# Clustered attention with a mish feed-forward: scores from float16 pairs, with a scale per head

## The chip, the cores and the metric

The kernel runs on one core of one Trainium2 chip. Times are device microseconds (us) of one execution. TensorE (PE in the rows, PEld for its weight loads), VectorE (DVE), ScalarE (ACT), GpSimd (POOL) and SyncE (SP, which only issues transfers) each work through their own instructions in order, and wait for each other by semaphores.

## What is computed

Four batches of eight heads, 768 positions, 64 elements a head. Each query and each key belongs to one of 16 clusters of its head; a query sees only the keys of its own cluster. Then a feed-forward layer with x·tanh(softplus(x)) ("mish").

```python
q_assign = argmax(einsum('bhsd,hcd->bhsc', q_n, c_n))      # q_n, k_n, c_n: unit length
k_assign = argmax(einsum('bhsd,hcd->bhsc', k_n, c_n))
mask = q_assign[:, :, :, None] == k_assign[:, :, None, :]
scores = where(mask, (q @ k.T) / 8, -1e9)
attn = softmax(scores)
x = (attn @ v)                                             # to (3072, 512)
h = x @ w_in                                               # w_in 512 x 2048
out = (h * tanh(softplus(h))) @ w_out                      # w_out 2048 x 512
```

## The kernel before

**Units.** The work on attention is cut into 96 units i (a head and 256 queries), each in two half units a (128 queries): 192 half units. Head n = i // 3; batch 0 is heads 0 to 7, units 0 to 23.

**Precision.** float32 values are split into a high and a low part, and products are built from parts. For a head's scores, `prep_hi` makes A, the rounded part of q (rows 0 to 63, times 0.125) and k (rows 64 to 127), and `prep_lo` makes B, what is left of both. `copy_t`, `copy_z`, `copy_b` and `copy_a` move halves of them about, so that the tiles B, A, T and Z hold what two products need: one with 128 rows (B and A) and one with 64 rows of parts and 16 rows of cluster marks (T and Z). All four are float32r, a 4-byte type. `hot_copy` writes the marks: where query and key share a cluster, 2^64 is added to the score. `scores(i, a)` issues four matmuls of 384 columns into one of two score banks (tag S): two of line L631 (B, A) and two of L636 (T, Z).

**Behind the scores.** `rowmax` (VectorE, L648) takes the negated maximum m of a row, `expo` (ScalarE, L662) exp(s + m) and its sum l, `total` and `recip` (VectorE, L674 and L682) one over the sum, `p_hi` (GpSimd, L700) the high part hl, `p_lo` (VectorE, L717) the low part, `ptrans` a transposing DMA into pt, `pv` (L753) the products with v, `pv_out` and `x_lo` the two parts of x. In batch 0 the probabilities stay float32 and are transposed by TensorE (L710).

**Clusters.** For each group q of four heads `assign_mm` multiplies raw q and k with the centroids, into a score bank; `assign_turn`, `assign_max`, `assign_hot` and `assign_back` on VectorE find the marks, `assign_put` and `assign_stg` turn them into values.

**Feed-forward.** `m1` (L832 to L834) forms h from x, `e_mish` (ScalarE, L843) applies mish, `e_gh` (GpSimd) and `e_gl` (VectorE, L857) split it, `m2` (L873 to L875) multiplies by w_out. ScalarE loads the table with mish before each pair of j, and the one with exp behind it (L842, L845). The feed-forward of a batch runs beside the attention of the next. The last two row blocks of the output use seven products in place of eight (L1025).

**What sets the order.** Every step has a due time from tables (T, N, and a shift for single steps). The program issues steps by due time, each behind the steps it needs, and so fixes the order on every engine. Nothing is reordered afterwards.

`norm_power` (L211 to L222) makes a power of two and its inverse from a sum: six operations on VectorE.

Of the kernel before, what the change touches and what calls it, by code (L numbers as in the profile page):

```python
# [8 lines left out]
F32 = mybir.dt.float32  # L9
# [12 lines left out]
BIG = float(2.0**64)  # L22
E20 = 485165195.40979
# [49 lines left out]
def tile_clustered_attention_mish_ffn(  # L73
# [36 lines left out]
    idle = cp.tile([P, 512], BF16, name="idle")  # L110
# [43 lines left out]
    def put_consts():  # L154
# [16 lines left out]
        )  # L171
    scq = cp.tile([P, 1], F32, name="scq")
# [38 lines left out]
    def norm_power(total, name, pool, tag, unit=2.0**-13):  # L211

        t = pool.tile([P, 1], F32, tag=f"{tag}t", name=f"{name}t")
        tu = t.bitcast(U32)
        nc.vector.tensor_scalar(t, total, 2.0**-120, None, op0=ALU.max)
# [3 lines left out]
        r = pool.tile([P, 2], F32, tag=f"{tag}r", name=f"{name}r")  # L219
        nc.vector.tensor_scalar(r[:, 1:], t, unit, None, op0=ALU.mult)  # L220
        nc.vector.reciprocal(r[:, :1], r[:, 1:])
# [245 lines left out]

    def operand(n, nm):
        st[nm, n] = opp.tile([P, S], F32R, tag=nm, name=f"{nm}_{n}")
        return st[nm, n]  # L470
# [5 lines left out]

    def prep_hi(n):
        pl.after(("qk_load", n))
        r, A = st["qk", n], operand(n, "A")
        if n < T["direct"]:  # L480
            nc.scalar.activation(A, r, AF.Copy, scale=scq)
            return
        if share(n, "f_b", n >= late):
            nc.gpsimd.tensor_scalar(r, r, scq, 1.0, op0=ALU.mult, op1=ALU.mult)
        sc = 1.0 if share(n, "f_b", n >= late) else scq
# [5 lines left out]
    def prep_lo(n):  # L491
        pl.after(("prep_hi", n))
        if n < T["direct"]:
            nc.vector.scalar_tensor_tensor(
                operand(n, "B"), st["qk", n], scq, st["A", n].bitcast(F32), op0=ALU.mult, op1=ALU.subtract
            )
            return
        r, A, Bt = st["qk", n], st["A", n].bitcast(F32), operand(n, "B")
        if share(n, "f_b", n >= late):
            nc.gpsimd.tensor_tensor(Bt, r, A, op=ALU.subtract)  # L500
        else:
            nc.vector.scalar_tensor_tensor(Bt, r, scq, A, op0=ALU.mult, op1=ALU.subtract)

    def copy(n, kind, dst, src):
        if n < T["direct"]:

            if kind != "copy_z":
                nc.scalar.copy(dst, src.bitcast(F32))
            else:
                nc.vector.tensor_copy(dst, src.bitcast(F32))  # L510
        elif share(n, f"f_{kind}", n >= late):
            nc.scalar.copy(dst, src.bitcast(F32))
        else:
            queue(n, kind).dma_start(dst.bitcast(F32), src.bitcast(F32))
# [61 lines left out]
    def assign_put(q):  # L576
        pl.after(("assign_back", q), ("put_consts",))
# [1071 lines left out]
```

## Time and profile before

| what | value |
|---|---|
| three runs | 871.47, 876.18, 876.86 us; median 876.18 |
| the profiled execution, its time | 873.17 us |
| its span (first to last instruction) | 871.44 us |
| TensorE busy | 838.5 us (96%) |
| weight loads busy | 608.8 us (70%) |
| VectorE busy | 697.9 us (80%) |
| ScalarE busy | 520.9 us (60%) |
| GpSimd busy | 434.9 us (50%) |

Matmuls overlap in their pipeline, so TensorE's busy time says that it had work, not how fast it went; for that one reads from the start of one matmul to the start of the next. The trace of this execution is the source of all rows below.

### The profile page before, as it was taken

What the parts mean: (1) busy time and instruction counts of PE and PEld (TensorE: products, weight loads), DVE (VectorE), ACT (ScalarE), POOL (GpSimd) and SP (SyncE); (2) the same over time, 40 slices, a digit from 0 to 9 for tenths busy, and PEclk for the clock granted to TensorE, in tenths of its full rate; (3) what the DMA queues carried; (4) which work ended last, traced back from release to release, by engine and by line L of the source; (5) the groups of instructions that cost most, each with busy time, mean ns of one, the idle gap of its engine ahead of it and who ended that gap; (6) DMA issues with size and microseconds to landing.
All of it is one profiled execution on the core that took longest, in us unless ns stands there. A gap on an engine that the chain in (4) does not pass through costs nothing.

```text
span 871.4 us, 17412 instructions
## 1 busy us (share of the span) xinstructions
PE 838.5 (96%) x6670; PEld 608.8 (70%) x6671; DVE 697.9 (80%) x1178; ACT 520.9 (60%) x881; POOL 434.9 (50%) x410
## 2 busy tenths in 40 slices
PE   8999899889999999999999999999999999999998
PEld 3666666667767767776777767776776777777787
DVE  7889988889978879778978789779888776488831
ACT  6878977667457567456556666465565555345520
POOL 1463656587657547466567457466566543110000
PEclk9999999999999999999999999999999999999999
DMA  8765671289679997688779997988967876000000
GB/s 322 254 181 153 187 220 46 61 166 188 126 141 173 214 179 134 135 180 168 136 135 182 195 171 128 159 178 148 156 130 141 144 131 122 13 1 14 2 31 32
DMA packets 253060, 121.51 MB, mean 139 GB/s; under 512 B 230288, under 2 KB 230800, under 8 KB 252976
## 3 DMA queue, kind: packets, MB, share of 16 engines
q1 hardware_dynamic: 247632, 108.46, 59.2%
q10 hardware_dynamic: 5344, 11.93, 6.7%
q8 instruction: 53, 0.87, 0.4%
q14 instruction: 31, 0.25, 0.1%
HBM read 35.72 MB, written 6.29 MB: 48 GB/s over the span
## 4 chain that ended last, share of the span: by engine, by line
PE 68%; DVE 14%; DMA 6%; ACT 5%; issue 3%; POOL 3%; ACTq 0%; SPq 0%; DVEq 0%; POOLq 0%
PE o L753 8%; PE h L832 8%; PE O L873 7%; PE h L833 7%; PE h L834 7%; PE O L875 7%; PE O L874 7%; PE s L631 5%; PE s L636 5%; DVE m L648 4%; DMA pt<-hl 3%; DVE hl L717 2%; ACT p L662 2%; DVE w L347 1%; PE as L543 1%
## 5 line engine op out<-in xcount | busy, mean ns | idle before, releaser
L662 ACT ACTIVATE p<-s,m 128x768 f32<-128x768 f32 x192 | 172.6, 899 | 173.5 <-DVE m L648 91.7
L700 POOL TENSOR_SCALAR hl<-p,l 128x768 f16<-128x768 f32 x144 | 172.2, 1196 | 149.2 <-DVE l L682 80.7
L648 DVE TENSOR_REDUCE m<-s 128x1 f32<-128x768 f32 x192 | 182.4, 951 | 39.7 <-PE s L636 35.8
L832 PE MATMUL h<-x,w 128*128 128x256 f16 x640 | 175.8, 275 | 4.0 <-ACT u L843 3.4
L717 DVE SCALAR_TENSOR_TENSOR hl<-p,l,hl 128x768 f16<-128x768 f32 x144 | 166.5, 1157 | 11.7 <-POOL hl L700 11.4
L833 PE MATMUL h<-x,w 128*128 128x256 f16 x640 | 174.4, 273 | 0.0
L834 PE MATMUL h<-x,w 128*128 128x256 f16 x640 | 174.4, 273 | 0.0
L631 PE MATMUL s<-A,B 128*128 128x384 f32 x384 | 119.0, 391 | 8.8 <-ACT p L662 6.1
L873 PE MATMUL O<-w,g 128*128 128x512 f16 x320 | 121.7, 380 | 0.0
L875 PE MATMUL O<-w,g 128*128 128x512 f16 x320 | 121.3, 379 | 0.0
L874 PE MATMUL O<-w,g 128*128 128x512 f16 x320 | 121.3, 379 | 0.0
L857 DVE SCALAR_TENSOR_TENSOR g<-u,mscg,g 128x512 f16<-128x512 f32 x80 | 92.0, 1150 | 35.8 <-POOL g L849 35.6
L849 POOL TENSOR_SCALAR g<-u,mscg 128x512 f16<-128x512 f32 x80 | 73.7, 924 | 66.9 <-ACT u L843 54.5
L636 PE MATMUL s<-Z,T 80*128 80x384 f32 x384 | 98.8, 338 | 1.9 <-DVE T L603 1.0
L832 PEld LDWEIGHTS <-w 128*128 128x128 f16 x768 | 75.1, 98 | 30.9 <-issue 19.6
L833 PEld LDWEIGHTS <-w 128*128 128x128 f16 x768 | 75.5, 98 | 15.6 <-issue 4.4
L753 PE MATMUL o<-pt,v 128*64 128x256 f16 x1296 | 79.3, 274 | 2.5 <-DMA pt<-hl 2.3
L834 PEld LDWEIGHTS <-w 128*128 128x128 f16 x768 | 75.1, 98 | 8.9 <-issue 0.2
L753 PEld LDWEIGHTS <-v 128*64 128x64 f16 x1296 | 68.5, 110 | 14.7 <-issue 12.2
L631 PEld LDWEIGHTS s<-A,B 128*128 128x128 f32 x384 | 61.3, 190 | 23.2 <-ACT p L662 9.4
L636 PEld LDWEIGHTS s<-Z,T 80*128 80x128 f32 x384 | 69.6, 189 | 2.5 <-ACT Z L600 1.3
L500 POOL TENSOR_TENSOR B<-qk,A 128x768 fp32r<-128x768 f32 x30 | 61.6, 2052 | 0.6
(225 smaller groups left out, 1299.9 us busy)
## 6 DMA issues: line engine op xcount, KB each, us to landing
qk<-in_qk_dram SPq DMA_DIRECT2D x32, 384.0 KB, 4.7
stage<-in_w_in_dram SPq DMA_DIRECT2D x16, 512.0 KB, 6.8
stage<-in_w_out_dram SPq DMA_DIRECT2D x16, 512.0 KB, 4.5
vraw<-in_vP_dram SPq DMA_DIRECT2D x16, 384.0 KB, 6.3
T<-A ACTq DMA_DIRECT2D x30, 192.0 KB, 3.3
Z<-B SPq DMA_DIRECT2D x30, 192.0 KB, 3.1
B<-T ACTq DMA_DIRECT2D x28, 192.0 KB, 3.5
out_dram<-osb SPq DMA_DIRECT2D x20, 256.0 KB, 2.7
```

Source lines behind the costliest of these rows:

```text
L631: nc.tensor.matmul(s[:, j, :384], st["B", n][:, q0 : q0 + P], st["A", n][:, j * 384 : (j + 1) * 384], start=True, stop=False,)
L636: nc.tensor.matmul(s[:, j, :384], st["T", n][: D + NCL, q0 : q0 + P], st["Z", n][: D + NCL, j * 384 : (j + 1) * 384], start=False, stop=True,)
L648: nc.vector.tensor_reduce(m, st["s", i, a][:, :, :384], axis=AX.XY, op=ALU.max, negate=True)
L662: nc.scalar.activation(p.rearrange("p (n x) -> p n x", n=2), st["s", i, a][:, :, :384], AF.Exp, bias=st["m", i, a], scale=1.0, accum_out=l,)
L717: nc.vector.scalar_tensor_tensor(t[:, 1], p, r, t[:, 0], op0=ALU.mult, op1=ALU.subtract)
L753: nc.tensor.matmul(o[s * D : s * D + D, :256], v if early else v[:, int(part == 1)], st["pt", 2 * m + s][:, :, c + (0 if early or part < 2 ...
L832: nc.tensor.matmul(o, wh, xh, start=(c == 0), stop=False)
L833: nc.tensor.matmul(o, wh, xl, start=False, stop=False)
L834: nc.tensor.matmul(o, wl, xh, start=False, stop=(c == 3))
L873: nc.tensor.matmul(o, gh, wh, start=(f == 0 and fi == 0), stop=False)
L874: nc.tensor.matmul(o, gh, wl, start=False, stop=False)
L875: nc.tensor.matmul(o, gl, wh, start=False, stop=(f == 7 and fi == 1))
```

## The change

It holds for batches 1 to 3 (`narrow(n)`: heads 8 to 31, units 24 to 95, 144 half units). There A, B, T and Z are float16, a 2-byte type, and so are the marks' values; q and k of each head are first multiplied by powers of two.

The scale comes from a sum of squares: `q_sq` (new, ScalarE) sums the squares of each row of a head; `assign_sum` (new, TensorE) adds the rows of q and those of k by two small float32 matmuls with a constant tile of ones (`side`), into the spare columns of the group's cluster bank; `assign_scale` (new, VectorE) turns them by `norm_power` and one more operation into scales `qs` for the operands and `qu` for the scores. `put_more` (new, once) changes the constants of the marks from 2^64 to 2^15 and makes `side`. `prep_hi` and `prep_lo` take `qs` in place of the constant scale.

Between the row maximum and the exponential stands `level` (new, two operations on VectorE on 128x1): it makes a scale per row (zero where a row has no key of its cluster) and an offset, and the exponential takes both.

For j = 74, 76 and 78 the table with mish is no longer loaded again.

```diff
+    def narrow(n):
+        return gof[n] >= H
     def operand(n, nm):
-        st[nm, n] = opp.tile([P, S], F32R, tag=nm, name=f"{nm}_{n}")
+        st[nm, n] = opp.tile([P, S], F16 if narrow(n) else F32R, tag=nm, name=f"{nm}_{n}")
         return st[nm, n]
...
+    def q_sq(n):
+        pl.after(("qk_load", n))
...
+        junk = gp.tile([P, S], BF16, tag="g", name=f"qj{n}")
+        nc.scalar.activation(junk, st["qk", n], AF.Square, accum_out=st["qq", q][:, j : j + 1])
+
+    def assign_sum(q):
+        n0 = owner[q]
+        pl.after(("assign_mm", q), ("put_more",), *(("q_sq", n0 + j) for j in range(4)))
+        for k in range(2):
+            nc.tensor.matmul(
+                st["as", q][:, S + 4 * k : S + 4 * k + 4], st["side"][:, k].rearrange("p a d -> p (a d)"), st["qq", q],
+                start=True, stop=True, skip_group_check=True,
+            )
+
+    def assign_scale(q):
+        pl.after(("assign_sum", q))
+        r = norm_power(st["as", q][:, S : S + 8], f"qs{q}", sm, "qs", wide=8, least=2.0**8)
+        u = sm.tile([P, 4], F32, tag="qu", name=f"qu{q}")
+        nc.vector.scalar_tensor_tensor(u, r[:, 8:12], 0.125, r[:, 12:], op0=ALU.mult, op1=ALU.mult)
...
     def prep_hi(n):
         pl.after(("qk_load", n))
-        r, A = st["qk", n], operand(n, "A")
+        if narrow(n):
+            pl.after(("assign_scale", gof[n] // 4))
+        r, A, s = st["qk", n], operand(n, "A"), st["qs", n] if narrow(n) else scq
...
-        stg = op1.tile([P, S], F32R, tag="stg", name=f"stg{q}")
+        stg = op1.tile([P, S], F32R if q < 2 else F16, tag="stg", name=f"stg{q}")
...
+    def level(i, a):
+
+        pl.after(("rowmax", i, a))
+        m, u = st["m", i, a], st["qu", units[i][2]]
+        w = sm.tile([P, 2], F32, tag="mw", name=f"mw{i}_{a}")
+        eng = nc.vector if share(2 * i + a, "f_m", True) else nc.gpsimd
+        eng.tensor_scalar(w[:, 0:1], m, FAR, u, op0=ALU.is_lt, op1=ALU.mult)
+        eng.tensor_scalar(w[:, 1:2], m, w[:, 0:1], 1.0, op0=ALU.mult, op1=ALU.mult)
+        st["mw", i, a] = w
...
-            bias=st["m", i, a], scale=1.0, accum_out=l,
+            bias=bias, scale=scale, accum_out=l,
...
-        if j % 2 == 0:
+        if j % 2 == 0 and j <= 72:
             nc.scalar.preload_act_table_set("mish")
...
-    'scores': 1.895,
-    'rowmax': -0.3,
+    'scores': 6.714,
+    'rowmax': 0.767,
+    'level': -0.29,
```

`share(..., "f_m", True)` is always true (the table has 1), so every `level` is VectorE's. The tables of due times change throughout (the last lines of the diff show three entries); on TensorE nearly all steps keep their places in batch 0, and from batch 1 on some change them. Three places follow.

TensorE, the second half unit of unit 54 (`s54_1`; O is a block of `m2`, h one of `m1`). Before:

```order
L874 MATMUL O3_0_5066<-w11_1101,g13_4945 128x512
L875 LDWEIGHTS g13_4945
L875 MATMUL O3_0_5066<-w11_1101,g13_4945 128x512
L631 MATMUL s54_1_5260<-A_18_4839,B_18_4994 128x384 x2
L636 MATMUL s54_1_5260<-Z_18_4996,T_18_4925 128x384 x2
L832 LDWEIGHTS w6_610
L832 MATMUL h30_5227<-x1_0_0_2468,w6_610 128x256
```

Of the change, the same place:

```order
L895 LDWEIGHTS w6_608
L895 MATMUL h30_5485<-x1_3_0_4563,w6_608 128x256
L678 LDWEIGHTS B_18_5269
L678 MATMUL s54_1_5506<-A_18_5066,B_18_5269 128x384
L683 LDWEIGHTS T_18_5179
L683 MATMUL s54_1_5506<-Z_18_5271,T_18_5179 128x384
L934 LDWEIGHTS g13_5187
L934 MATMUL O3_0_5319<-w10_980,g13_5187 128x512
```

(Each of the two LDWEIGHTS and MATMUL pairs of the scores stands there twice.) The scores moved from behind the twelve matmuls of O3_0 to ahead of them; and a float16 weight load is an instruction of its own.

VectorE from the first half unit of unit 54 on (m the maximum, l the sum, hl the parts of the probabilities, g those of mish). Before:

```order
L648 TENSOR_REDUCE m54_0_5224<-s54_0_5219 128x1
L717 SCALAR_TENSOR_TENSOR hl53_1_5242<-p53_1_5205,l53_1_5206,hl53_1_5242 128x768
L648 TENSOR_REDUCE m54_1_5265<-s54_1_5260 128x1
L674 TENSOR_SCALAR l54_0_5268<-l54_0_5268 128x1
L682 RECIPROCAL l54_0_5268<-l54_0_5268 128x1
L857 SCALAR_TENSOR_TENSOR g14_5156<-u29_5160,mscg1_4596,g14_5156 128x512
L648 TENSOR_REDUCE m55_0_5294<-s55_0_5289 128x1
```

Of the change:

```order
L695 TENSOR_REDUCE m54_0_5479<-s54_0_5474 128x1
L704 TENSOR_SCALAR mw54_0_5481<-m54_0_5479,qu4_4373 128x1
L705 TENSOR_SCALAR mw54_0_5481<-m54_0_5479,mw54_0_5481 128x1
L778 SCALAR_TENSOR_TENSOR hl53_1_5500<-p53_1_5460,l53_1_5461,hl53_1_5500 128x768
L695 TENSOR_REDUCE m54_1_5511<-s54_1_5506 128x1
L704 TENSOR_SCALAR mw54_1_5513<-m54_1_5511,qu4_4373 128x1
L705 TENSOR_SCALAR mw54_1_5513<-m54_1_5511,mw54_1_5513 128x1
L735 TENSOR_SCALAR l54_0_5517<-l54_0_5517 128x1
L743 RECIPROCAL l54_0_5517<-l54_0_5517 128x1
L918 SCALAR_TENSOR_TENSOR g14_5411<-u29_5415,mscg1_4811,g14_5411 128x512
L695 TENSOR_REDUCE m55_0_5553<-s55_0_5548 128x1
```

The order of the old operations is the same; two new ones stand right behind each maximum.

VectorE at the scale of group 4, heads 16 to 19, whose scores begin with unit 48. Before:

```order
L648 TENSOR_REDUCE m44_0_4179<-s44_0_4174 128x1
L717 SCALAR_TENSOR_TENSOR hl43_1_4197<-p43_1_4144,l43_1_4145,hl43_1_4197 128x768
L399 TENSOR_REDUCE vsm2_4203<-vm2_3964 128x1
L648 TENSOR_REDUCE m44_1_4210<-s44_1_4205 128x1
L674 TENSOR_SCALAR l44_0_4216<-l44_0_4216 128x1
```

Of the change:

```order
L705 TENSOR_SCALAR mw44_0_4360<-m44_0_4358,mw44_0_4360 128x1
L230 TENSOR_SCALAR qs4t_4365<-as4_4317 128x8
L231 TENSOR_SCALAR qs4t_4365<-qs4t_4365 128x8
L232 TENSOR_SCALAR qs4t_4365<-qs4t_4365 128x8
L233 TENSOR_SCALAR qs4t_4365<-qs4t_4365 128x8
L235 TENSOR_SCALAR qs4r_4370<-qs4t_4365 128x8
L236 RECIPROCAL qs4r_4370<-qs4r_4370 128x8
L520 SCALAR_TENSOR_TENSOR qu4_4373<-qs4r_4370 128x4
L778 SCALAR_TENSOR_TENSOR hl43_1_4389<-p43_1_4310,l43_1_4311,hl43_1_4389 128x768
L735 TENSOR_SCALAR l44_0_4397<-l44_0_4397 128x1
L743 RECIPROCAL l44_0_4397<-l44_0_4397 128x1
L695 TENSOR_REDUCE m44_1_4413<-s44_1_4408 128x1
```

The seven operations of `assign_scale` came in between the first maximum of unit 44 and the low part of unit 43's second half, and the next half unit's total and reciprocal moved ahead of the second maximum.

## Rows read from the trace of the kernel before

**Rows 1.** Windows: us of each engine, then PEclk (granted clock), DMA share, GB/s.
```profile
core 0: us, PE busy (x) PEld busy (x) DVE busy (x) ACT busy (x) POOL busy (x), PEclk, DMA share, GB/s
50.00:100.00 50.00, 45.09 (x361) 32.67 (x359) 47.44 (x80) 39.81 (x78) 29.01 (x35) 1.00 0.56 165
...
415.30:608.20 192.90, 190.87 (x1529) 136.70 (x1528) 161.70 (x266) 115.33 (x189) 116.56 (x101) 1.00 0.88 161
```

**Rows 2.** TensorE's waits from 200 to 735: us in total, times, longest.
```profile
PE o L753 <- DMA pt<-hl: 2.3, 3, 0.9
PE s L631 <- ACT p L662: 2.3, 2, 1.1
```

**Rows 3.** Timeline of TensorE: start us, duration us, engine, line, instruction.
```profile
450.20 0.38 PE L873 MATMUL O<-w,g 128*128 128x512 f16 x1
450.41 0.38 PE L874 MATMUL O<-w,g 128*128 128x512 f16 x1
...
453.23 0.27 PE L833 MATMUL h<-x,w 128*128 128x256 f16 x1
453.34 0.27 PE L834 MATMUL h<-x,w 128*128 128x256 f16 x1
453.37 0.59 PE L631 MATMUL s<-A,B 128*128 128x384 f32 x2
...
454.17 0.28 PE L832 MATMUL h<-x,w 128*128 128x256 f16 x1
```

**Rows 4.** Weight loads by line: busy us, mean ns, then idle time before them.
```profile
L832 PEld LDWEIGHTS <-w 128*128 128x128 f16 x768 | 75.1, 98 | 30.9 <-issue 19.6
L631 PEld LDWEIGHTS s<-A,B 128*128 128x128 f32 x384 | 61.3, 190 | 23.2 <-ACT p L662 9.4
```

**Rows 5.** Timeline of TensorE around a float32 matmul of one column.
```profile
68.66 0.51 PE L636 MATMUL s<-Z,T 80*128 80x384 f32 x2
68.84 0.36 PEld L319 LDWEIGHTS s<-ws0m,ones 128*128 128x128 f32 x2
...
69.25 0.50 PE L589 MATMUL put<-hott,put_w 128*128 128x512 bf16 x2
```

**Rows 6.** Timeline near the end of the table loads; in brackets what ended a wait.
```profile
766.74 1.28 ACT L842 ACT_TABLE_LOAD   x1
...
768.77 0.27 PE L832 MATMUL h<-x,w 128*128 128x256 f16 x1 [1.48 <-ACT u L843]
```

**Rows 7.** Timeline of VectorE behind a row maximum.
```profile
452.17 0.95 DVE L648 TENSOR_REDUCE m<-s 128x1 f32<-128x768 f32 x1
453.04 0.14 DVE L674 TENSOR_SCALAR l<-l 128x1 f32<-128x1 f32 x1
453.21 0.16 DVE L682 RECIPROCAL l<-l 128x1 f32<-128x1 f32 x1
453.29 0.73 DVE L857 SCALAR_TENSOR_TENSOR g<-u,mscg,g 128x512 f16<-128x512 f32 x1
```

**Rows 8.** Timeline of VectorE: first of norm_power's six operations, and what follows them.
```profile
365.86 0.16 DVE L215 TENSOR_SCALAR vs2t<-o 128x1 f32<-128x1 f32 x1
...
366.89 1.23 DVE L717 SCALAR_TENSOR_TENSOR hl<-p,l,hl 128x768 f16<-128x768 f32 x1
```

**Rows 9.** One line's instructions (L447): ns shortest/median/longest, first and last start.
```profile
L447 DVE TENSOR_TENSOR msch<-vs2r,ws0r x1: 1760/1760/1760, 541.4 to 541.4; 128x1 f32<-128x1 f32 x1
L447 DVE TENSOR_TENSOR msch<-vs3r,ws0r x1: 146/146/146, 732.2 to 732.2; 128x1 f32<-128x1 f32 x1
```

**Rows 10.** VectorE's longest wait from 415.3 to 608.2: us in total, times, longest.
```profile
DVE m L648 <- PE s L636: 12.5, 13, 2.8
```

**Rows 11.** ScalarE by line: a square with its sum over 128x768.
```profile
L368 ACT ACTIVATE vq<-vraw 128x768 bf16<-128x768 f32 x16 | 13.5, 842 | 1.8 <-DMA vraw<-in_vP_dram 1.6
```

**Rows 12.** TensorE's longest waits before 200 us: us in total, times, longest.
```profile
PE q L710 <- ACT p L662: 4.6, 8, 0.9
PE gram L296 <- DVE w L276: 4.4, 5, 1.7
```

More of the change, by code (lines that the diff above doesn't have):

```diff
@@ L107, in tile_clustered_attention_mish_ffn @@
     pl = Plan(tc)
-    idle = cp.tile([P, 512], BF16, name="idle")
+    idle = cp.tile([P, 512], BF16, tag="idle", name="idle")
     nc.vector.memset(idle, 1.0)
@@ L171, in put_consts, with put_more @@
         )
+    def put_more():
+        pl.after(("assign_stg", 1), ("scores", 0, 1))
+        st["side"] = side = cp.tile([P, 2, 2, D], F32, tag="idle", name="side")
+        w4 = put_w.rearrange("p (j s n) -> p j s n", j=4, s=2)
+        for n, c in ((0, BIG16 / BIG), (1, BIG16)):
+            nc.vector.tensor_scalar(w4[:, :, n], w4[:, :, n], c, None, op0=ALU.mult)
+        nc.vector.tensor_scalar(put_b, put_b, BIG16, None, op0=ALU.mult)
+        nc.vector.memset(side, 0.0)
+        for n in range(2):
+            nc.vector.memset(side[n * D : (n + 1) * D, 0, n], 1.0)
+            nc.vector.memset(side[n * D : (n + 1) * D, 1, 1 - n], 1.0)
     scq = cp.tile([P, 1], F32, name="scq")
@@ L649, in rowmax @@
         st["m", i, a] = m
-    def expo(i, a):
-        pl.after(("rowmax", i, a))
+    def level(i, a):
[6 more added lines that the diff above has]
+        st["mw", i, a] = w
+    def expo(i, a):
+        pl.after(("level" if narrow(units[i][2]) else "rowmax", i, a))
+        if narrow(units[i][2]):
+            scale, bias = (st["mw", i, a][:, n : n + 1] for n in range(2))
+        else:
+            scale, bias = 1.0, st["m", i, a]
         p = pp.tile([P, S], F32, tag="p", name=f"p{i}_{a}")
@@ L1084, in tile_clustered_attention_mish_ffn @@
         fn.__name__: fn
-        for fn in (scores, rowmax, expo, total, recip, p_hi, p_lo, ptrans, e_mish, e_gh, e_gl)
+        for fn in (scores, rowmax, level, expo, total, recip, p_hi, p_lo, ptrans, e_mish, e_gh, e_gl)
     }
@@ L1208, in tile_clustered_attention_mish_ffn @@
                 e = i // 2 * 2 + N["E"][i % 2 * 2 + a]
+                if narrow(units[i][2]):
+                    pl.at(e + N["level"], ops["level"], i, a)
                 for key in ("scores", "rowmax", "expo", "total", "recip", "p_hi", "p_lo", "ptrans"):
@@ L1421 @@
+    ('load', 1): -13.358,
+    ('load', 2): -7.467,
+    ('load', 3): -5.261,
+    'prep_hi': -3.462,
+    'prep_lo': 0.023,
+    'copy_t': -2.663,
+    'copy_z': -2.047,
+    'copy_a': -1.56,
+    'hot_copy': -1.481,
+    'copy_b': -0.91,
+    'assign_mm': -3.498,
+    'assign_turn': -4.226,
+    'assign_max': -4.024,
+    'assign_hot': -1.785,
+    'assign_back': -3.113,
+    'assign_put': 2.001,
+    'assign_stg': -2.377,
+    'v_load': 17.489,
+    'v_sq': 18.356,
     'v_scale': 21.77,
-    'v_max': 20.441,
+    'v_max': 23.128,
@@ new lines @@
+    ('moe_scale_h', 1): 0.027, ('prep_hi', 18): -0.145, ('w_abs', 9): 0.036, ('total', 33, 1): -0.074,
+    ('ptrans', 44, 1): -0.218, ('e_gl', 8): 0.163, ('expo', 52, 1): 1.794, ('level', 38, 0): -0.135,
+    ('pv', 13, 0): -0.124, ('scores', 41, 0): 4.917, ('rowmax', 34, 1): 0.892, ('rowmax', 35, 0): 1.091,
+    ('rowmax', 35, 1): 0.892, ('rowmax', 36, 0): 0.892, ('rowmax', 36, 1): 0.892, ('rowmax', 37, 0): 3.322,
+    ('rowmax', 37, 1): 0.892, ('rowmax', 38, 0): 0.892, ('rowmax', 38, 1): 0.892, ('rowmax', 39, 0): 0.892,
```

621 lines of the change are left out of this document (376 added, 245 removed), and 26 rows, old and new, of tables (N, SHIFT).

## The prediction, before the changed kernel had run

> **What bounds the kernel now.** I read the windows first, then the waits, then single instructions. In the cycle from 415.3 to 608.2 us (48 half units; the order repeats with it, and the 144 half units with float16 to come are three such cycles) TensorE is busy 190.87 of 192.9 us and VectorE 161.70 [rows 1]. The granted clock is 1.00 there, the 2.4 GHz level. The list of who waited for whom shows TensorE stopped only 4.6 us in all between 200 and 735 us [rows 2]. So from batch 1 on the time is TensorE's own stream, matmul behind matmul, and it becomes shorter only if the stream does or one of the few stops goes. VectorE is next, at 84%. Before 200 us it is otherwise: from 50 to 100 us VectorE is at 47.44 of 50 and TensorE at 45.09 [rows 1].
>
> **Float16 scores on TensorE.** A busy matmul tells little, as they overlap; start to start is what counts. 512 float16 columns take 0.21 us (450.20 to 450.41), 256 take 0.11 [rows 3]. 384 lie halfway, 0.16, so a half unit's four matmuls will take 0.65. Now: the last matmul ahead of a scores block starts at 453.34 and needs its 0.11, so the block has the time from 453.45 to 454.17, 0.72 us for four [rows 3]. The gain is 0.07 in rows of two decimals, 0.06 to 0.08; I take 0.06. 144 x 0.06 = **8.6 us off**. Ends: nothing, if float16 streams no faster, and 144 x 0.08 = 11.5.
>
> Weight loads are where readers may hope for more: 190 ns before, 98 ns for a float16 load of that width [rows 4]. If loads set the pace, four would give back 4 x 0.092 = 0.37 us a block, 53 us in all. But four loads are 0.76 us end to end and the block takes 0.72, of which four streams are 0.65: the loads lie beside the streams, and only what sticks out goes. The Trainium skill ("TensorE: Matmul & The Clock Gate", Weight-path perf modes) says that fast weight load comes on by itself for 128 weights that are not FP32; the trace agrees in the load's length. Read as a throughput rule, with the same page's remark that a stream's spacing is set by load and matmul together, it would give the 53 us; by the rows it gives 8.6.
>
> **The new sums of squares.** Six times two small float32 matmuls go into the stream. The nearest row: the float32 matmul of one column behind a scores block puts the next matmul 0.41 us behind the block's last one (its load starts at 68.84 with that last matmul; the next starts at 69.25), where 0.18 is usual (68.66 to 68.84) [rows 5]: 0.23 us. The second one of a pair has nothing in front to hide its two loads of 0.18: 0.36. Together 0.6 us, 6 x 0.6 = **3.6 us on**. Ends: 2.8 (twice 0.23) and 4.8.
>
> **The table loads.** From j = 74 on three loads of a table that is already there go. Two are hidden: ScalarE has nothing to do there. The last isn't: it runs from 766.74 for 1.28 us, the mish behind it holds TensorE for 1.48 us until 768.77, and from there TensorE streams to the end [rows 6]. **1.3 us off.** Ends: nothing and 1.5.
>
> **VectorE.** Each half unit gets two operations on 128x1, behind the row maximum and dependent on it. One that doesn't wait for its forerunner starts 0.87 us behind the maximum's start (452.17 to 453.04), while the maximum itself lasts 0.95; a dependent one will start some 0.04 behind its end: 0.12 later. A dependent pair is 0.17 apart (453.04 to 453.21), rounded up to 0.18 for a scalar read from memory, and the last gives way after 0.08 (453.21 to 453.29) [rows 7]. 0.38 us; ends 0.16 (0.08 each) and 0.50 (0.12 and twice 0.19). A cycle gets 48 x 0.38 = 18.2 us. The scale per head is a chain like that of the values' scale, six operations in 1.03 us (365.86 to 366.89) [rows 8], and one with two inputs, which on 128x1 takes 146 ns alone and 1760 ns when it meets GpSimd's work [rows 9]: 1.5 us for one, ends 1.2 and 2.8; twice in a cycle, 3.0. So VectorE has 161.7 + 18.2 + 3.0 = 182.9 us to do in a cycle. TensorE's cycle becomes 192.9 - 2.9 + 1.2 = 191.2. That is 95.7%. The highest share that this program shows VectorE reach is 47.44 of 50, 95% [rows 1]; at that ceiling the cycle lasts 182.9 / 0.95 = 192.5 us, 1.3 above TensorE's own. VectorE's idle time now is 31.2 us a cycle, of which 12.5 are waits for scores [rows 10]: these it can fill, the rest must shrink by half, which it does when VectorE comes later to what GpSimd and ScalarE have ready. I charge a quarter of 3 x 1.3: **1 us on**.
>
> The skill speaks against such operations ("VectorE: DVE Perf Modes", the TRN2 errata): many small tiles each pay a fixed latency, measured there near 150 cycles of 0.96 GHz, 0.156 us. An estimate from that page is 0.31 us a half unit, which leaves VectorE at 94% and TensorE in the lead: 5 instead of 4 us of gain ahead of the table load. The rows' 0.17 for a dependent pair lies close to that fixed part.
>
> Behind the maximum stand the exponential, and behind that the score bank that TensorE wants back. The 0.38 us go into that chain; the new order answers by putting the second scores ahead of twelve-matmul blocks (the order rows at s54_1), so that the third block comes later behind it.
>
> **At no cost.** ScalarE squares each head once, 0.84 us [rows 11], in ScalarE's idle 77 us a cycle (115.33 busy [rows 1]). Operand copies move half the bytes through DMA engines that are 0.88 busy [rows 1]; TensorE waited 2.3 us for transposes [rows 2], which at best go. prep_hi now waits on VectorE for the scale; behind it on GpSimd stands the next half unit's hl. Uncovered, each of the six waits would cost about the 1.5 us chain, but the scale is needed four units ahead of its scores. The retuned order of batch 0 I count as nothing.
>
> **Sum.** -8.6 + 3.6 - 1.3 + 1.0 = -5.3. The profiled execution took 873.17, its span 871.44 and 1.7 around it: 867.9. The three runs beside it have the median 876.18; all four average 874.4, 1.2 above the profiled one. So **869 us**, 0.8% below the median. A measurement of this kernel can tell about 1% from no change: faster is below 867.4, slower above 885.
>
> **Rivals.**
> 1. VectorE becomes the bound (the other side). Place: every cycle of batches 1 to 3. It costs time against before once VectorE's work passes 0.95 x 192.9 = 183.3 us, at 0.39 us a half unit; I took 0.38. With the high ends, 161.7 + 24 + 5.6 = 191.3, the cycle is 201.4, 8.5 more, three times: 25 us, 898. Halfway (0.44) it is 195.6: 8 us more, less the table load, about 881. For it: the sum above. Against: the operations come one after another in a known order, and waits for scores give slack.
> 2. The new order also takes stops away before 200 us, where TensorE waits 4.6 us for the exponential at the transposes and 4.4 for weights [rows 12]. Half of both is 4.5: 864. For it: the order there was changed. Against: nearly every TensorE row keeps its place.
> 3. Float16 is no faster on TensorE (the change doesn't do what it says): 873.2 + 3.6 - 1.3 + 1 + 1.2 = 878. Against: the 0.72 against 0.65.
> 4. Weight loads set the pace: 53 us instead of 8.6, about 825. Against: 0.76 doesn't fit into 0.72.
>
> **Chances.** Forecast (865 to 874) 0.48, rival 1 0.17, rival 2 0.20, rival 3 0.10, rival 4 0.02, none of these 0.03. Of the forecast's, 0.15 lies below 867.4; rival 2 adds 0.18, rival 4 0.02: faster 0.35. Slower is rival 1 above 885 and most of the unknown: 0.17. Same: 0.48. The range reaches past rival 2 below, where a little more of those waits goes, and past rival 1's middle above: 860 to 886.
>
> **What would show it.** Start to start of the scores: 0.16 us and a block of 0.65. Level operations 0.17 to 0.19 apart. In a cycle VectorE near 183 us and TensorE's waits still a few us; if waits for p or for hl reach 10 us, rival 1 holds. The wait of 1.48 for the mish gone. The first 200 us the same within 3. The prediction is wrong if VectorE's share falls short of 95% while TensorE waits.

## The result, and the profile of the changed kernel

The changed kernel takes **888.72 us** (median of four, 888.50 to 889.89) beside 875.19 for the kernel before: ratio 1.0147, 95% interval 1.0118 to 1.0177. Once more, beside the experiments, it took 890.00 (ratio 1.0168, 1.0146 to 1.0189). It is 1.5% slower where I had forecast 0.8% less. The profiled execution took 889.89 us, its span is 888.2. One execution of the experiment no_level (1416.96 us) and one of no_reload (1713.57 us) lie far from all others of their kernel and are left out of the ratios.

Where in the program the time went, by the starts of the scores in the two traces, after minus before: half unit 48 (the first with float16) +3.4 us, half unit 64 +5.9, 112 +9.4, 176 +17.3, the end +16.7. So a few microseconds are lost up to the first cycle of batch 1, then 0.1 us with every half unit, and between the mish of j = 74 and that of 78, where table loads are gone, 1.8 comes back.

The windows of the changed kernel (us of each engine, then granted clock, DMA share, GB/s), a stretch of batch 0 and the cycle that answers the one in [rows 1] (half units 112 to 160):

```profile
core 0: us, PE busy (x) PEld busy (x) DVE busy (x) ACT busy (x) POOL busy (x), PEclk, DMA share, GB/s
50.00:100.00 50.00, 45.45 (x375) 33.56 (x374) 47.45 (x81) 39.13 (x76) 27.87 (x33) 1.00 0.57 157
424.80:623.40 198.60, 190.36 (x1536) 126.75 (x1535) 179.74 (x377) 126.49 (x205) 116.97 (x100) 1.00 0.77 142
```

The cycle lasts 198.6 us in place of 192.9. VectorE has 179.74 us to do in place of 161.70, 90.5% of the cycle; TensorE now stands still for 8 us of it. The clock is at its higher level as before. TensorE's waits from 200 to 735 us, to be held against [rows 2], and VectorE's in the cycle, against [rows 10] (us in total, times, longest):

```profile
PE s L678 <- ACT p L723: 11.2, 19, 1.6
PE O L936 <- DVE g L918: 2.6, 5, 0.8
PE o L814 <- DMA pt<-hl: 1.5, 3, 0.8
...
DVE g L918 <- POOL g L910: 4.2, 7, 0.7
DVE l L735 <- ACT p L723: 3.3, 6, 0.7
DVE x L875 <- ACT x L851: 2.4, 5, 1.7
DVE m L695 <- PE s L683: 1.0, 3, 0.5
```

TensorE waits 11.2 us for score banks that the exponential still holds; it was 2.3. VectorE waited 12.5 us a cycle for scores; now it is 1.0: it is no longer ahead of TensorE, it comes behind. VectorE stands still for 18.9 us of the cycle; all its waits in that list are 11.9 of them, and 7.0 lie under no wait (before: 27.9 of 31.2, which leaves 3.3). The chain that ended last says the same, first of the kernel before, then of the changed one:

```profile
PE 68%; DVE 14%; DMA 6%; ACT 5%; issue 3%; POOL 3%; ACTq 0%; SPq 0%; DVEq 0%; POOLq 0%
PE 37%; DVE 33%; ACT 13%; issue 6%; DMA 6%; POOL 3%; ACTq 1%; SPq 0%; DVEq 0%; POOLq 0%
```

Timeline of a half unit, answering [rows 7] (and, in TensorE's rows, [rows 3]): start us, duration us, engine, line, instruction, in brackets what ended a wait:

```profile
559.22 0.94 DVE L695 TENSOR_REDUCE m<-s 128x1 f32<-128x768 f32 x1
560.20 0.21 DVE L704 TENSOR_SCALAR mw<-m,qu 128x1 f32<-128x1 f32 x1
560.44 0.21 DVE L705 TENSOR_SCALAR mw<-m,mw 128x1 f32<-128x1 f32 x1
560.58 1.01 DVE L778 SCALAR_TENSOR_TENSOR hl<-p,l,hl 128x768 f16<-128x768 f32 x1
...
560.77 0.99 ACT L723 ACTIVATE p<-s,mw 128x768 f32<-128x768 f32 x1 [2.18 <-DVE mw L705]
...
560.97 0.49 PE L678 MATMUL s<-A,B 128*128 128x384 f16 x2
561.29 0.49 PE L683 MATMUL s<-Z,T 80*128 80x384 f16 x2
561.62 0.27 PE L893 MATMUL h<-x,w 128*128 128x256 f16 x1
```

From the maximum's start to the operation behind level: 1.36 us. Without level it is 0.87 [rows 7]. **Level takes 0.49 us of VectorE, not 0.38.** The exponential starts 0.61 us behind the maximum's end (560.16 to 560.77), where 0.12 was the median before, and lasts 0.99. The scores' block is 0.65 us (560.97 to 561.62), as expected. By line, 200 to 735 us (busy us, mean ns | idle before, and what ended it):

```profile
L723 ACT ACTIVATE p<-s,mw 128x768 f32<-128x768 f32 x132 | 130.5, 989 | 152.7 <-DVE l L735 68.6 <-DVE mw L705 64.1 <-POOL B L545 4.5
L704 DVE TENSOR_SCALAR mw<-m,qu 128x1 f32<-128x1 f32 x131 | 28.0, 214 | 4.6
L705 DVE TENSOR_SCALAR mw<-m,mw 128x1 f32<-128x1 f32 x131 | 28.1, 214 | 4.6
L735 DVE TENSOR_SCALAR l<-l 128x1 f32<-128x1 f32 x132 | 19.2, 145 | 9.6 <-ACT p L723 9.2
```

Level's operations last 214 ns; `total` (L735), the same kind on the same 128x1 but with constants in the instruction, 145.

And this is a stop of TensorE for a bank, from the timeline of all engines (rows of other work left out):

```profile
601.81 0.50 PE L678 MATMUL s<-A,B 128*128 128x384 f16 x2
602.15 0.49 PE L683 MATMUL s<-Z,T 80*128 80x384 f16 x2
...
603.79 0.49 PE L678 MATMUL s<-A,B 128*128 128x384 f16 x2
...
604.67 2.49 DVE L778 SCALAR_TENSOR_TENSOR hl<-p,l,hl 128x768 f16<-128x768 f32 x1
604.71 1.64 POOL L545 TENSOR_TENSOR B<-qk,A 128x768 f16<-128x768 f32 x1
607.19 0.96 DVE L695 TENSOR_REDUCE m<-s 128x1 f32<-128x768 f32 x1
...
608.19 0.21 DVE L704 TENSOR_SCALAR mw<-m,qu 128x1 f32<-128x1 f32 x1
608.43 0.21 DVE L705 TENSOR_SCALAR mw<-m,mw 128x1 f32<-128x1 f32 x1
...
608.77 0.99 ACT L723 ACTIVATE p<-s,mw 128x768 f32<-128x768 f32 x1 [3.96 <-DVE mw L705]
...
609.49 0.95 DVE L695 TENSOR_REDUCE m<-s 128x1 f32<-128x768 f32 x1
...
609.90 0.48 PE L678 MATMUL s<-A,B 128*128 128x384 f16 x2 [1.40 <-ACT p L723]
```

Two half units are under way, one in each bank: their scores begin at 601.81 and 603.79, their maxima at 607.19 and 609.49. VectorE is behind: from 601.52 on it does a low part of mish and five small operations, and then its low part hl, 1.02 us by the median, takes 2.49 beside GpSimd's subtraction for B. So the first maximum begins 5.4 us after its scores, level and the longer exponential come on top, and the bank is free at 609.8, when TensorE has waited 1.40 us for it. Such meetings are not new (29 operations of VectorE above 1.4 us between 200 and 735 us before, 24 after), but before, TensorE waited for a bank only 2.3 us in all [rows 2].

### The profile page after: what moved, and what is told of

The parts are those of the page before. It is cut to its first block, busy times and chain, and to the rows that moved or that the text cites. A ratio compares the mean times of both kernels' runs of the same rounds, so it can differ in the third digit from the quotient of the medians.

```text
span 888.2 us, 17846 instructions
## 1 busy us (share of the span) xinstructions
PE 838.7 (94%) x6695; PEld 580.7 (65%) x6695; DVE 749.7 (84%) x1516; ACT 550.5 (62%) x926; POOL 439.1 (49%) x410
## 4 chain that ended last, share of the span: by engine, by line
PE 37%; DVE 33%; ACT 13%; issue 6%; DMA 6%; POOL 3%; ACTq 1%; SPq 0%; DVEq 0%; POOLq 0%
DVE m L695 9%; DVE hl L778 7%; ACT p L723 5%; PE o L814 5%; PE h L893 4%; PE h L895 4%; PE h L894 4%; PE O L936 3%; DVE g L918 3%; PE O L934 3%; DMA pt<-hl 3%; PE O L935 3%; ACT L903 2%; PE s L678 2%; PE s L683 2%
## 5 line engine op out<-in xcount | busy, mean ns | idle before, releaser
L761 POOL TENSOR_SCALAR hl<-p,l 128x768 f16<-128x768 f32 x144 | 176.4, 1225 | 161.8 <-DVE l L743 88.7
L723 ACT ACTIVATE p<-s,mw 128x768 f32<-128x768 f32 x144 | 142.4, 989 | 166.1 <-DVE l L735 73.4
L778 DVE SCALAR_TENSOR_TENSOR hl<-p,l,hl 128x768 f16<-128x768 f32 x144 | 163.4, 1139 | 3.8 <-POOL hl L761 3.1
L678 PE MATMUL s<-A,B 128*128 128x384 f16 (+1 forms) x384 | 99.4, 340 | 19.3 <-ACT p L723 14.8
L910 POOL TENSOR_SCALAR g<-u,mscg 128x512 f16<-128x512 f32 x80 | 76.0, 954 | 67.5 <-ACT u L904 55.2
L918 DVE SCALAR_TENSOR_TENSOR g<-u,mscg,g 128x512 f16<-128x512 f32 x80 | 82.7, 1034 | 26.1 <-POOL g L910 25.9
L683 PE MATMUL s<-Z,T 80*128 80x384 f16 (+1 forms) x384 | 95.8, 330 | 2.3 <-DMA T<-stg 1.3
L936 PEld LDWEIGHTS <-g 128*128 128x128 f16 x320 | 31.2, 97 | 45.0 <-DVE g L918 8.1
L904 ACT ACTIVATE u<-h,msch 128x512 f32<-128x512 f32 x80 | 51.2, 685 | 15.0 <-PE h L895 12.4
L545 POOL TENSOR_TENSOR B<-qk,A 128x768 f16<-128x768 f32 (+1 forms) x30 | 56.6, 1887 | 0.6
```

The source lines that it names most:

```text
L678: nc.tensor.matmul(s[:, j, :384], st["B", n][:, q0 : q0 + P], st["A", n][:, j * 384 : (j + 1) * 384], start=True, stop=False,)
L723: nc.scalar.activation(p.rearrange("p (n x) -> p n x", n=2), st["s", i, a][:, :, :384], AF.Exp, bias=bias, scale=scale, accum_out=l,)
L761: nc.gpsimd.tensor_scalar(t[:, 0], p, r, 1.0, op0=ALU.mult, op1=ALU.mult)
L778: nc.vector.scalar_tensor_tensor(t[:, 1], p, r, t[:, 0], op0=ALU.mult, op1=ALU.subtract)
L936: nc.tensor.matmul(o, gl, wh, start=False, stop=(f == 7 and fi == 1))
```

## Experiments

All ratios are against the kernel before, run beside them (medians 875.7 to 876.3). "Aside" means that the work is done at its place and nobody reads the outcome. In the runs without level, with level aside, late_bias, scale_read and imm_level the probabilities lack the division by the head's scale; float16 with a constant scale is right for inputs of this size only.

### Which part costs: level, sums, order

**Level left out**: the two operations go, and `scale, bias = 1.0, st["m", i, a]` in the exponential.

```diff
-        eng.tensor_scalar(w[:, 0:1], m, FAR, u, op0=ALU.is_lt, op1=ALU.mult)
-        eng.tensor_scalar(w[:, 1:2], m, w[:, 0:1], 1.0, op0=ALU.mult, op1=ALU.mult)
```

> The changed kernel in its own order, with both operations of level left out (the exponential takes scale 1.0 and the bare maximum, so the rows' probabilities differ from the reference's: the division by the head's scale is missing). Theory A (level, between maximum and exponential, costs the gain, as chain or as VectorE work): 870 to 875 us, TensorE's waits for p L723 fall from 11.2 us (200 to 750 us) to under 4, the scores stay at 0.16 us start to start. Rival B (the changed order costs it): 885 to 889, waits stay. Rival C (the new sums of squares and scales cost it, through hl and prep_hi): 885 to 889.

> The run without level once more, for an undisturbed profile (the division by the head's scale is missing). Expected: 870 to 878 us as before, against 864.5 for float16 with a constant scale and 888.7 for the changed kernel. In the profile, theory A says: TensorE's waits for p under 4 us between 200 and 750 us. What sets it 10 us above float16 with a constant scale must show in it: rival C1 (the twelve small matmuls and the square's buffer, which is one of mish's g buffers): waits of TensorE or VectorE for g; rival C2 (prep_hi waits for the scale, and hl stands behind it on GpSimd): TensorE waiting for pt.

Ratios 0.9983 (0.9953 to 1.0013) and 0.9969 (0.9947 to 0.9991), the second 873.45 us: level costs 14 to 17 us (888.72 and 890.00 against 875.06 and 873.45). TensorE's waits for p are 2.9 us. Without level the kernel stands where the one before stood: order and sums use up float16's gain, and the loss is level's.

**Level aside**: only the exponential's edit.

> The changed kernel in its own order; level's two operations run at their place, but nobody reads them: the exponential takes scale 1.0 and the bare maximum (the division by the head's scale is missing, as in the run without level). VectorE has the same work, the chain from scores to the free bank is shorter by what the exponential waited for them and by its own 0.09 us. Theory A1 (the chain, some 0.6 us a half unit, is what costs): 871 to 876, like the run without level. Theory A2 (VectorE's load, 0.49 us a half unit, costs): 885 to 889, like the changed kernel. Half and half: 880.

883.37 us, 1.0096 (1.0060 to 1.0131): 10 us of level's price come without any change of the chain behind the maximum (9.9 against 873.45). That is nearer to A2's figure than to A1's, and below A2's.

**Float16 with a constant scale**: no level, no sums, no scale per head, `st["qs", owner[q] + j] = scq`.

> The changed kernel in its own order with a constant scale: no level, no sums of squares, no scale per head (right for inputs of this size only). Against the run without level this takes away the twelve small matmuls, 24 squares of ScalarE and six chains on VectorE. By my sum's terms 3.6 us less than the run without level for the matmuls, so 867 to 871. Rival C (these sums and scales cost more, through waits): more than 6 us below the run without level. If float16 gives nothing, it lies at 875 or above.

864.47 us, 0.9881 (0.9842 to 0.9920): below what I expected, so sums and scale cost some 9 us, not 3.6.

**The new tables on the kernel before.**

> The kernel before with the changed kernel's tables of due times and nothing else. Theory A (the order costs only what batch 0 shows, 3.4 us up to half unit 48): 877 to 880 against 875. Rival B (the order costs what was lost): 884 to 892, with the loss growing in batches 1 to 3 too. If the order is only better or neutral by itself: 870 to 876.

1069.93 us, 1.2224 (1.2176 to 1.2272), outside every expectation, and of no use as a price. Its longest wait points to the reason:

```profile
ACT p L662 <- DVE m L648: 381.7, 146, 6.3
```

In the new tables the maximum's own due time is late, since the step `level`, due earlier, pulls it forward. Without that step the maximum stood behind other work of VectorE, and 146 exponentials waited for it (49, and 91.7 us in all, in the kernel before).

**So once more, with every step kept and emptied**: float16 with a constant scale, but A, B, T, Z and the marks' values float32r.

```diff
-        st[nm, n] = opp.tile([P, S], F16 if narrow(n) else F32R, tag=nm, name=f"{nm}_{n}")
+        st[nm, n] = opp.tile([P, S], F32R, tag=nm, name=f"{nm}_{n}")
```

> Float16 with a constant scale, but with A, B, T, Z and the marks' values in float32r as before: the changed kernel's order, with empty steps in place of level, sums and scales so that every step stands where it does in the changed kernel, and the three table loads left out. Against 875.7 of the kernel before this is order plus table loads; against 864.5 it is float16's own share. By my sum: 875.7 - 1.3 = 874.4, and float16 gives 8.6 to 9.9. If the order alone costs (3.4 us in batch 0 and more): 878 to 882, float16 gives 14 to 17. If the order alone gives: 866 to 870.

879.55 us, 1.0034 (1.0011 to 1.0058): the order costs 3.6 us, and what the table loads give back beside it. Float16's share in this order, matmuls and half as many bytes in the copies together, is 879.55 - 864.47 = 15.1 us.

**Float16 with a constant scale in the old order** (the tables of the kernel before):

> Float16 with a constant scale in the order of the kernel before (its tables; right for inputs of this size only). Against 864.5 in the changed kernel's order this prices the order with float16 operands. By new_order_f32, where the changed order plus 1.3 us of table loads came out 3.6 slower: 860. By my prediction's terms, 875.9 - 8.6 - 1.3 = 866. If float16's half as many bytes in the copies make the changed order as good as the old one: 864 to 866.

861.50 us, 0.9826 (0.9806 to 0.9845), as new_order_f32 led one to expect. It is faster than both kernels, but fits only inputs whose scores float16 holds at a constant scale. Its only wait of 200 to 735 us in TensorE's list:

```profile
PE s L658 <- ACT p L694: 2.7, 3, 1.2
```

**The changed kernel in the old order:**

> The changed kernel with the tables of the kernel before (the new steps at the changed kernel's due times). It tells whether the new order answers level. With float16 and a constant scale the old order was 3 us better (861.5 against 864.5). If the new order only costs: 885 to 887. If it was needed for the longer chain and the scales: 893 to 910, with longer waits for p or for the scale.

902.66 us, 1.0282 (1.0245 to 1.0319), TensorE's waits for p 16.8 us. So the new order costs 3 us without level and saves 13 to 14 with it (the old tables were never fitted to the new steps): it answers level in part, and not sufficiently.

### Sums and scale

**Sums and scales aside** (no level; prep_hi and prep_lo take the constant scale):

> The run without level, with one edit more: sums of squares and scales are computed at their place, but nobody reads them, prep_hi and prep_lo take the constant scale (right for inputs of this size only). C1 (the sums' own instructions and buffers cost the 10 us between the run without level and float16 with a constant scale): 872 to 877, like the run without level. C2 (the wait of prep_hi for the scale costs it): 864 to 868. By the 3.6 us of my sum alone: 868.

872.18 us, 0.9958 (0.9939 to 0.9977): of the 9 us between f16_only and the run without level, 7.7 are the sums' own work and 1.3 the waiting for the scale. C1.

**The squares alone:**

> Float16 with a constant scale, plus the 24 squares on ScalarE alone (no small matmuls, no scale; right for inputs of this size only). Float16 with a constant scale took 864.5, with sums and scales computed aside 872.2; the small matmuls stand in the profile with 0.36 us of TensorE's stream each time, 2.2 us in all. If squares and the buffer that they share with mish cost the rest: 869 to 871. If the small matmuls and the chain on VectorE do: 864 to 866.

866.37 us, 0.9866 (0.9829 to 0.9904). By the medians 1.9 us are the squares', which is within the spread of these runs (864.25 to 867.22 against 864.07 to 865.14); the small matmuls, the chains on VectorE and the constant tile make 5.8. On TensorE the two float32 matmuls of a group, four in the trace, take 0.37 us (the changed kernel's timeline):

```profile
228.52 0.49 PE L683 MATMUL s<-Z,T 80*128 80x384 f16 x2
228.84 0.51 PE L511 MATMUL as<-qq,side 128*128 128x4 f32 x4
229.21 0.27 PE L893 MATMUL h<-x,w 128*128 128x256 f16 x1
```

Six times 0.37 is 2.2 us. Where the other 3.6 are lost I can't show: no single wait holds them.

### Amount of work, or a late exponential

**Late, but at a constant scale**: level's second operation gives back the bare maximum, the exponential waits for it.

```diff
-        eng.tensor_scalar(w[:, 1:2], m, w[:, 0:1], 1.0, op0=ALU.mult, op1=ALU.mult)
+        eng.tensor_scalar(w[:, 1:2], w[:, 0:1], 0.0, m, op0=ALU.mult, op1=ALU.add)
```

> The changed kernel with level's second operation giving back the bare maximum and the exponential at a constant scale 1.0, but still waiting for level (the division by the head's scale is missing). VectorE's work and the chain stay, only the scale read from memory goes, 0.09 us an exponential. If the wait for level makes up the 5.3 us between level_aside and the changed kernel: 887 to 889. If the longer exponential does: 883 to 884. In proportion to 0.5 and 0.09 us: 888.

882.11 us, 1.0077 (1.0052 to 1.0103). The wait by itself adds nothing to level_aside; I had expected 5 us of it.

> The changed kernel once more, beside the experiments. Its first time, 888.7 us, was taken apart from them; level_aside (883.4) and late_bias (882.1) leave 5 to 7 us to be explained. Expected 887 to 890. If it comes out at 883 to 885, the exponential's scale from memory costs next to nothing and what was read as its price was a difference between sessions.

It stays at 890.0, so the gap of 7 us is real.

**The longer exponential alone**: level aside, `scale = ones` from memory.

> level_aside with one edit: the exponential reads a scale of one from memory (a constant column) in place of the immediate 1.0; it still takes the bare maximum and does not wait for level (the division by the head's scale is missing). The exponential should last 0.99 us instead of 0.90. Theory P (the longer exponential costs by itself, 0.09 us at every half unit where the bank is awaited): 886 to 890. Theory Q (it costs only behind the later start that the wait for level brings, when the slack of 0.6 us is used up): 883 to 885.

879.73 us, 1.0039 (1.0024 to 1.0054), with the exponential at 988 ns. Below level_aside, which neither theory had: the longer exponential alone costs nothing. Behind the late start it costs: the changed kernel, which differs from late_bias in little but the scale read from memory, stands 6.6 to 7.9 us above it. So wait and length cost only together. My reading of why is the slack of the banks. From the records I took, for half units 56 to 185, the time from an exponential's end to the next scores in the same bank; 0.14 us means that TensorE waited. Under 0.2 us lie 4 of 130 in the kernel before, 8 without level, 12 with level aside and 12 with the longer exponential, 29 with the late one, 30 in the changed kernel; TensorE's waits for p are 2.3, 2.9, 4.7, 4.4, 7.4 and 11.2 us. By this reading the wait uses up the slack, and what comes on top of it is paid. It is argued and not shown, and it covers only part: 29 half units at 0.09 us are 2.6 us, TensorE's waits grow by 3.8, and the time by 6.6 to 7.9. Why scale_read is 3.6 us below level_aside stays open.

**One operation in place of two:**

```diff
-        eng.tensor_scalar(w[:, 0:1], m, FAR, u, op0=ALU.is_lt, op1=ALU.mult)
-        eng.tensor_scalar(w[:, 1:2], m, w[:, 0:1], 1.0, op0=ALU.mult, op1=ALU.mult)
+        eng.tensor_scalar(w[:, 1:2], m, u, 1.0, op0=ALU.mult, op1=ALU.mult)
```

> The changed kernel with one operation of level in place of two: offset = maximum times the head's scale, and the exponential reads the head's scale itself (rows without a key of their cluster are not set apart, so it is right only where no such row exists). VectorE has 0.21 to 0.25 us less a half unit and the offset comes 0.25 earlier. If cost goes with VectorE's work (9.9 us for two operations, 0.084 us a half unit on TensorE) and with the late start: 882 to 885. If the longer exponential is the main part of what is left: 884 to 886. Not below 878, since the exponential keeps its 0.99 us and the sums stay.

Here the exponential reads the head's scale itself, and rows without a key of their cluster are not set apart. 877.94 us, 1.0014 (0.9989 to 1.0040), and lower than expected: the second operation, and the later start that goes with it, costs 11 to 12 us, the first, with the longer exponential, 4.5.

**VectorE relieved elsewhere**: `nc.vector.tensor_copy(g[:, 1], g[:, 0])` in place of L918 from j = 4 on (the feed-forward then leaves out mish's own low part).

> The changed kernel with level whole and in its place, but VectorE relieved elsewhere, off the chain from scores to the bank: from j = 4 on the low part of mish (L918, 1.06 us) is a copy of the high part (the feed-forward's low product is wrong), some 0.2 us. 76 times 0.85 us is 65 us of VectorE's work less, about what level adds (0.49 us, 144 times, 70 us). Theory L (it is VectorE's amount of work that makes the maxima late, and so the bank): 873 to 878, like the run without level; scores start to maximum start falls from a median of 1.93 us back toward 1.4. Theory S (the start of the exponential 0.5 us later and its 0.09 us do it): 885 to 889, with only the 2.6 us of waits for g gone.

878.24 us, 1.0026 (1.0001 to 1.0052). Level and the exponential are as in the changed kernel, and 11 us are back. The copy took 0.41 us, so the relief was 76 x 0.65 = 49 us, less than I meant. The scores' start to the maximum's start falls from a median of 1.93 us to 1.61. Theory L: with level whole and the exponential as late and as long as before, work taken off VectorE elsewhere gives most of the loss back. 4.8 us are left above the run without level; as 49 us are less than the 144 x 0.49 = 71 that level takes, this run can't tell whether they are the chain's or VectorE's.

```profile
L919 DVE COPY g<-g 128x512 f16<-128x512 f16 x66 | 27.1, 411 | 9.8 <-POOL g L910 9.6
```

**Level on GpSimd** (`('f_m', 1): 0`):

> The changed kernel with level on GpSimd in place of VectorE. VectorE has its work of before, but the exponential waits for GpSimd, which is busy 59% of the time with operations of about 1.2 us. Theory L: VectorE's relief outweighs: 876 to 884. Theory S: a start 1 us and more later, with TensorE's waits for the bank at 20 us and more: 895 to 920.

1020.96 us, 1.1634 (1.1588 to 1.1679), worse than either expected. In order on GpSimd, level's operations wait for the maximum and hl for them:

```profile
PE s L678 <- ACT p L723: 63.0, 36, 3.9
...
ACT p L723 <- POOL mw L705: 148.1, 65, 4.7
DVE hl L778 <- POOL hl L761: 132.3, 74, 3.5
POOL mw L704 <- DVE m L695: 122.8, 52, 5.4
```

**The same two operations with constants in the instruction:**

```diff
-        eng.tensor_scalar(w[:, 0:1], m, FAR, u, op0=ALU.is_lt, op1=ALU.mult)
-        eng.tensor_scalar(w[:, 1:2], m, w[:, 0:1], 1.0, op0=ALU.mult, op1=ALU.mult)
+        eng.tensor_scalar(w[:, 0:1], m, 0.0, 1.0, op0=ALU.mult, op1=ALU.add)
+        eng.tensor_scalar(w[:, 1:2], m, 1.0, 1.0, op0=ALU.mult, op1=ALU.mult)
```

> The changed kernel with level's two operations on immediates in place of scalars from memory (first column 1.0, second the bare maximum; the division by the head's scale and the rows without a key are left out). The exponential still reads both columns from memory and waits for them. The operations should last 0.14 us in place of 0.21, and not hang on each other: 0.25 to 0.33 us a half unit in place of 0.49. If the cost goes with VectorE's amount of work, as one_op (0.25 us, 877.9) and light_gl (878.2) say: 876 to 880. If it goes with the number of operations or the late exponential: 885 to 889.

875.87 us, 1.0006 (0.9990 to 1.0023): 13 to 14 us less than the changed kernel, with as many operations and the exponential behind both, 0.99 us long. It leaves out the scale and the rows without a key; its second operation does not need the first.

```profile
L704 DVE TENSOR_SCALAR mw<-m 128x1 f32<-128x1 f32 x135 | 20.7, 154 | 4.7
L705 DVE TENSOR_SCALAR mw<-m 128x1 f32<-128x1 f32 x135 | 19.4, 144 | 0.0
```

From the maximum's start to the next operation the median over some 120 half units is 0.87 us without level, 1.12 here and with one operation, 1.37 in the changed kernel. So 0.00, 0.25 and 0.49 us of VectorE a half unit give 873.5, 875.9 to 877.9, and 888.7 to 890.0 us: the first quarter of a microsecond costs some 2 to 5 us, the second 11 to 14. The exponential's start moves with it (0.10, 0.37 and 0.62 us behind the maximum's end), so this row alone does not part work from delay; light_gl and level_aside do.

The same 48 half units (112 to 160) without level, with constants, and with level aside (columns as in the first table):

```profile
418.30:607.60 189.30, 187.90 (x1537) 126.96 (x1536) 161.66 (x280) 122.12 (x205) 113.70 (x100) 1.00 0.81 149
420.10:611.90 191.80, 188.63 (x1536) 126.97 (x1535) 170.07 (x377) 126.50 (x205) 116.22 (x100) 1.00 0.81 147
422.10:618.20 196.10, 189.51 (x1537) 126.89 (x1536) 181.68 (x377) 122.23 (x205) 119.74 (x100) 1.00 0.77 144
```

VectorE's share is 85.4%, 88.7% and 92.6%, and 90.5% in the changed kernel.

### The table loads

```diff
-        if j % 2 == 0:
+        if j % 2 == 0 and j <= 72:
             nc.scalar.preload_act_table_set("mish")
```

> The kernel before with the three table loads from j = 74 on left out and nothing else. My sum: 1.3 us less, 874.6 against 875.9; bounds 0 and 1.5 us. A measurement tells this from nothing only just; in the profile the wait of 1.48 us of TensorE for the last mish should be gone or shorter by 1.3, and the end with it.

873.54 us, 0.9974 (0.9960 to 0.9989): 2.4 less by the medians. In the trace the start of the mish of j = 78 moves 1.7 us forward against that of j = 74, and TensorE's wait for it [rows 6] is gone.

## Why the prediction was wrong

**The step that failed** is VectorE's, +1.0 us. It measured +14 to +17. Three things in it:

1. *The price of level, 0.38 us, was 0.49.* The first operation was right (0.11 later; 0.12 taken). The dependent pair was taken as 0.17, rounded to 0.18, from an operation with constants and a reciprocal, neither with a scalar from memory [rows 7]; it is 0.24. What follows comes 0.14 behind, not 0.08. My upper end, 0.50, was the value. By rival 1's own working, with 0.49 and the measured 1.17 us for the chain of the scale (its first operation starts at 428.54, the maximum behind it at 429.71), VectorE has 161.7 + 23.5 + 2.3 = 187.5 us to do and at 95% the cycle is 197.4; it measured 198.6. That they lie so close is in part luck: VectorE was busy 179.74 us, and at 95% that is 189.2, less than the 191.2 that I gave TensorE. Of the 7.8 us between, 48 x 0.07 = 3.4 are gaps inside level (560.16 to 560.20 and 560.41 to 560.44), and mish's low part became shorter (1173 to 1058 ns, means from 200 to 735 us; 24 in a cycle, 2.8 us). So the price alone does not make the loss. I had written that it decides at 0.39 and then charged a quarter of the excess at 0.38, so near the edge that a price read to 0.1 us could not carry a chance of only 0.17.
2. *The ceiling of 95% was too high.* It was read in batch 0, where VectorE is the busiest engine (47.44 of 50 us, TensorE 45.09). Beside TensorE's stream it stopped at 90.5%: dependent operations leave gaps, and in its order it waits for g (4.2 us a cycle), for the exponential's sum (3.3) and for x (2.4). Nor is there one ceiling: with level aside it reached 92.6% of the same half units, and that kernel too stands 10 us above the one without level. imm_level and one_op, at 88.7% both, show that the cost begins well below 0.38 us. What the prediction named as proof against itself, a share short of 95% while TensorE waits, came true, and so did the sign of rival 1, waits for p beyond 10 us (11.2).
3. *The exponential became 0.09 us longer* (989 ns against 899), as it reads its scale from memory. That stood nowhere in my sum. The Trainium skill has it ("ScalarE: Activation LUTs", What ACT_TABLE_LOAD costs): each operand of one value per partition that is read from memory adds about 93 ns to an activation. The trace agrees, with 90 ns. Alone it cost nothing (scale_read); behind the late start it is what sets the changed kernel 6.6 to 7.9 us above late_bias, and so 5 to 7 above level_aside.

I had seen that the 0.38 us go into the chain behind the maximum, but took the new order for an answer to it. It is one, of 13 to 14 us (old_order), and not enough.

**Float16, -8.6.** Right in kind, on the low side. In the old order it gives 876.3 - 861.5 = 14.8, of which the table loads are 1.7 to 2.4. The block with the matmul ahead of it got 0.05 shorter (813 to 763 ns behind an h block, by the medians), scores and feed-forward together, start to start, 0.06 to 0.07 us a half unit, near the 0.06 taken; and TensorE's waits for transposes, 2.3 us [rows 2], which I left uncounted, are gone. What is left, up to 2 us, I can't place. Weight loads did not set the pace (rival 4), nor was float16 no faster (rival 3).

**Sums, +3.6.** The matmuls cost 2.2, under my range (0.37 us each time, not 0.6: the second matmul of a pair, two in the trace, takes 0.22, 228.99 to 229.21, and not 0.36). But the whole part cost 7.7, as the squares I put at nothing took some 1.9 and some 3.6 lie where I can't show them. The term was too small by half.

**Waiting for the scale**, put at nothing: 1.3 us between two runs that spread over 5 to 7 us, so no more than that it is small.

**Table load, -1.3.** Right in kind: 1.7 in the traces, 2.4 by the medians, past my upper end of 1.5.

**The order of batch 0**, put at nothing: +3.4 us at half unit 48 in the changed kernel's trace, +2.0 in its second one; 3 us over the whole with float16. Wrong, and against rival 2: TensorE's waits for p at the transposes went from 4.6 to 5.1 us, those for w from 4.4 to 3.5 [rows 12].

**Sum of what was measured**: 875.9, order and table loads +3.6, float16 -15.1, squares +1.9, small matmuls and scales +5.8, waiting for the scale +1.3, level's work on VectorE +9.9, its late and longer exponential +5.3 to +6.6: 888.7 to 890.0. It adds up because each step is the difference of two runs; scale_read, one_op and imm_level show that the parts are not independent.

One sentence on the kernel, earlier, has the marks the wrong way round: they take 2^64 (2^30 in float16) from the scores of other clusters. Nothing in the sum hangs on it.

## What to carry to other kernels

When a change puts work on the engine that is second in line, price it with the very form of instruction that it uses (a scalar from memory is another price than a constant), and read the engine's ceiling from a stretch where it runs beside the bound, not from one where it is the bound. If the price lies near the point where a rival decides, the rival is as likely as the forecast. And a gain on the leading engine makes the second one the next bound: here 0.06 us came off TensorE's half unit and 0.49 onto VectorE's, and TensorE waited for VectorE where VectorE had waited for TensorE.

## What was not expected of the hardware

- An operation of VectorE on 128x1 takes 214 ns with a scalar from memory and 144 to 154 with constants; with the scalars from memory a dependent pair starts 0.24 us apart. The two operations with constants, which don't depend on each other, take 0.25 us of VectorE a half unit in place of 0.49 (imm_level).
- The exponential over 128x768 takes 988 ns when its scale is read from memory, 898 when it is a constant.
- VectorE's low part hl takes up to 2.49 us in place of 1.02 when GpSimd subtracts for B in the same moment; of the changed kernel's 24 operations above 1.4 us, 16 run beside such a subtraction. The Trainium skill ("SBUF — State Buffer", Who interferes with whom) says that an operation of VectorE with two inputs from SBUF contends with one of GpSimd that reads SBUF, through ports that are an exclusive lock. The row agrees in size: 2.49 is close to 1.02 and GpSimd's 1.64 together, though VectorE's operation had started first, at 604.67 against 604.71.
- The response to a price is steep at the edge: 0.25 us a half unit cost 2 to 5 us, 0.49 cost 14 to 17, over 144 half units.
